# Grouped-query attention over a key and value cache on one core: the last row of wo's second half loaded by heads, and two V loads whole

## The chip, the core and the metric

The kernel runs on one of the eight cores of a Trainium2 chip. The metric is the device time of one execution in microseconds (us). A core has TensorE (PE, with its weight loads as PEld), VectorE (DVE), ScalarE (ACT), GpSimd (POOL) and SyncE (SP). SP and ACT issue the transfers from HBM, which 16 DMA engines carry out.

## The reference

Eight batches of four tokens ask 32 query heads, which share 8 heads of a cache of 2048 keys. All data is bf16.

```python
B, Sq, D = 8, 4, 512
Hq, Hkv, Sk, Dh = 32, 8, 2048, 128
q = (x @ wq).reshape(B, Sq, Hq, Dh).transpose(0, 2, 1, 3)
k = jnp.repeat(k_cache, Hq // Hkv, axis=1)
v = jnp.repeat(v_cache, Hq // Hkv, axis=1)
scores = jnp.einsum("bhqd,bhkd->bhqk", q, k) * (Dh ** -0.5)
p = softmax(scores)
o = jnp.einsum("bhqk,bhkd->bhqd", p, v)
out = o.transpose(0, 2, 1, 3).reshape(B, Sq, Hq * Dh) @ wo
```

k_cache and v_cache are 33.5 MB each, wq and wo 4.2 MB each.

## The kernel before

The work is cut into eight units `u`, each of which reads 4 MB of K and 4 MB of V. Units 1 to 6 (`single(u)`) are one batch with its eight heads; units 0 and 7 are four heads of the last two batches. All large loads go through `ring`, four slots of 4 MB, two members of 2 MB each. Loads are taken in the order k0, wq, k1, v0, k2, v1, ..., k7, v6, v7, wo, and a load goes into the slot of the load four before it, once that one's readers are done. `issue(done)` issues as many as fit; SP works them off in order, so a load that waits for its slot holds up the ones behind it. `load_kv` (L110) issues one load in parts: `by_member` makes two transfers of 2 MB, `whole` one of 4 MB, and `by_half` two of 2 MB, each with half of the keys of both members. The list `split` (L155) names the loads that go by member: V of units 0 to 4 and K of unit 7. V of unit 7 goes by half, the others are whole.

A unit runs so. DVE transposes K from the ring (`turn`, L213), PE multiplies it with the queries (`scores`, L251), DVE takes the maxima (`top`, L264), ACT the exponentials (L291), DVE turns them (L305), ACT, POOL and DVE copy them into a block-diagonal form (L315), and PE multiplies them with V (`values`, L331). Each matmul of L331 reads a key of both members of V at once. The result is scaled (L343, L351, L353), and PE orders it by tokens into a PSUM tile (`by_tokens`, L375).

The end is the product with wo. wo has 4096 rows of 512 numbers: 32 query heads of 128 rows. It comes as two halves `gg` of 16 heads, each into one member of the ring's slot. A partition holds 16 rows (`RW`), which are 16 successive rows of wo, so that eight partitions (`DG`) hold a head. `load_wo` (L141) issues the first half as one transfer of 2 MB, and the second in four parts by the rows of a partition, 0 to 7, 8 to 12, 13 and 14, and 15.

`to_rows(gg, n)` (L384) copies the attention output of a half out of PSUM (L389), and DVE transposes it, `n` rows at a time, into `oP[gg]` (L394): `oP[gg][:, r, :]` has, for each partition, the column of the output that belongs to its row `r` of wo. `project(gg, r0, r1)` (L399) then multiplies row after row, two matmuls each (L403), adding up in PSUM. The order at the end is: `to_rows(0, 16)` between the two parts of the last `values`; `project(0, 0, 4)`; `to_rows(1, 4)`, four transposes; `project(0, 4, 16)`; `project(1, 0, 16)`. Each row waits only for the transfer that has it and for its transpose. DVE and ACT then evict the two halves of the sum (L482, L483), and SP stores 32 KB (L484).

Of the kernel before, what the change touches and what calls it, by code (L numbers as in the profile page):

```python
# [17 lines left out]
def kernel(  # L18
# [9 lines left out]
    nc = tc.nc  # L28

    B, Sq, D = x.shape  # L30
    _, Hkv, Sk, Dh = k_cache.shape
    HqDh = wq.shape[1]
    Hq = HqDh // Dh
    rep = Hq // Hkv
    T = B * Sq
    R = D // 128
    G = 4
    S = 128 // G
    C = Sk // S
    NG = Hkv // G  # L40
    NB = 2
    NU = B * Hkv // (G * NB)
# [10 lines left out]
    DH = D // 2  # L53
    RW = 16
    DG = Dh // RW
    scale = float(Dh) ** -0.5
    assert Dh == 128 and C == 64 and Q == 16 and NB * Q == 32 and NT == 4 and NU == B == 8
    assert NS == NG == NB and NS1 == B - NB
# [14 lines left out]
    ring = ring_pool.tile([128, NR, NB, C * Dh], BF16, name="ring")  # L73
# [9 lines left out]
    oP = [const.tile([128, RW, T], BF16, name=f"oP{i}") for i in range(NG)]  # L83
# [17 lines left out]
    def take(key):  # L101
        slot_of[key] = n_loads[0] % NR
        n_loads[0] += 1
        return slot_of[key]
# [35 lines left out]

    def load_wo():  # L141
        slot = take("wo")
        for gg, cuts in ((0, (0, RW)), (1, (0, 8, 13, 15, RW))):
            rows = wo[gg * G * 512 : (gg + 1) * G * 512, :].rearrange("(p r) j -> p (r j)", r=RW)
            for r0, r1 in zip(cuts, cuts[1:]):
                nc.sync.dma_start(ring[:, slot, gg, r0 * D : r1 * D], rows[:, r0 * D : r1 * D])

    loads = ["k0", "wq", ("k", 1)]
    for u in range(NU):
# [2 lines left out]
            loads.append(("k", u + 2))  # L152
    loads.append("wo")
    loads.reverse()
    split = [("v", 0), ("v", 1), ("v", 2), ("v", 3), ("v", 4), ("k", NU - 1)]  # L155

    def issue(done):

        while loads and n_loads[0] < done + NR:
            what = loads.pop()  # L160
            if what == "k0":
                load_kv("k", 0, by_member, (nc.sync, nc.scalar))
                nc.sync.dma_start(x_sb[:, :], x.flatten_outer_dims())
            elif what == "wq":
                load_wq()
            elif what == "wo":
                load_wo()
            elif what in split:
                load_kv(*what, by_member)
            else:  # L170
                load_kv(*what, by_half if what == ("v", NU - 1) else whole)
# [11 lines left out]
    for r, b in ((r, b) for r in range(rep) for b in range(NB)):  # L183
        nc.gpsimd.tensor_copy(
            out=perm[:, r, W0 : W0 + 128]
            .rearrange("k (g x) -> k g x", g=G)[:, :, : NB * Sq]
            .rearrange("k g (b s) -> k b g s", b=NB)[:, b],
            in_=by_row[:, r, b],
        )
    for b in range(NB):  # L190
        nc.vector.tensor_reduce(
            out=of_b[:, b : b + 1],
            in_=ident[:, :].rearrange("k (g b q) -> k b g q", g=G, b=NB)[:, b],
# [190 lines left out]
    def to_rows(gg, n):  # L384

        o_r = q_sb[:, gg, :, :, :, :].rearrange("k r j w e -> k (r j w e)")
        half = rep * Dh // 2
        for i, copy in enumerate((nc.scalar.copy, nc.vector.tensor_copy)):
            copy(  # L389
                out=o_r[:, i * half : (i + 1) * half].rearrange("k (h d) -> k h d", d=Dh),  # L390
                in_=o_pms[i][:, :, gg, :],
            )
        for r in range(0, RW, n):
            nc.vector.transpose(  # L394
                out=oP[gg][:, r : r + n, :],
                in_=o_r.rearrange("k (h g r) -> k r h g", h=rep, r=RW)[:, r : r + n],
            )

    def project(gg, r0, r1):  # L399
        w = ring[:, slot_of["wo"], gg, :].rearrange("p (r j) -> p r j", r=RW)  # L400
# [19 lines left out]
    for gg in range(NG):  # L420
        psq = psum_o.tile([128, rep * Dh], FP32, tag="o", name="psq")
        for r in range(R):
# [10 lines left out]
            out=q_sb[:, gg, :, :, :, :].rearrange("t r j w e -> t (r j w e)"), in_=psq[:, :]  # L433
        )
        for i in range(rep):
            nc.vector.transpose(  # L436
                out=qT[:, gg, :, :, i, :, :].rearrange("w j b s e -> w j b (s e)").bitcast(FP32),
                in_=q_sb[:, gg, i, :, :, :].rearrange("t j w e -> t (j w e)").bitcast(FP32),
# [3 lines left out]
    for u in range(NU + 1):  # L442
# [19 lines left out]
        if u >= 1:  # L462
            values(u - 1, 0)
            if u == NU:
                joined(u - 2)
                by_tokens(u - 2)
                to_rows(0, RW)
            values(u - 1, 1)
            scaled(u - 1)
            if u == NU:  # L470
                joined(u - 1)
# [4 lines left out]
    project(0, 0, 4)  # L476
    by_tokens(NU - 1)
    to_rows(NG - 1, RW // 4)
    project(0, 4, RW)
    project(1, 0, RW)  # L480
# [34 lines left out]
```

## Time and profile before

| What | Value |
|---|---|
| Timed runs | 184.68, 190.56 and 191.4 us; median 190.56 us |
| Profiled execution | 184.38 us, of which the span of instructions 182.5 us |
| Busy: PE, DVE, ACT, POOL | 75%, 71%, 39%, 22% |
| Read from HBM | 75.53 MB, 414 GB/s over the span |
| DMA queues, share of 16 engines | SP's (q1) 94.3%, ACT's (q10) 2.8%, instructions (q8) 0.2% |
| Mean granted PE clock | 0.963 |
| wo's five transfers, KB and us to landing | 2048: 25.9, 1024: 28.2, 640: 29.1, 256: 29.3, 128: 28.0 |
| Store of the output | 32 KB, 1.5 us to landing |

The profile is one execution as the hardware profiler took it. Its span runs from the first to the last instruction; the rest of the execution's time lies around it. A line such as `L403 PE MATMUL s_ps<-ring,oP` is a line of the kernel, an engine, an operation, and the tiles that it writes and reads. In brackets behind it stands the time that the engine sat idle before it, and what ended that. A share of DMA is the mean busy share of the 16 engines in the stretch; a packet counts by its start, so a short stretch can show a little over 1. "Us to landing" runs from the issue of a transfer to its completion, so it has in it the time behind earlier transfers in the queue.

### The profile page before, as it was taken

The numbers are of one execution on the slowest core, as the hardware profiler recorded it, in microseconds if no ns is written. First come the engines' busy times: TensorE is split into PE (matmuls) and PEld (weight loads), VectorE is DVE, ScalarE is ACT, GpSimd is POOL, SyncE is SP. The second block draws the span as 40 slices with busy tenths as digits, with TensorE's granted clock in tenths as the row PEclk, the third lists the DMA queues.
The fourth block names the chain that finished last, engine by engine and source line by source line (L and its number), as shares of the span: only waits on it lengthen the run. The fifth ranks groups of instructions, "written<-read, shape, count | busy, mean of one in ns | idle before, by whom it ended". The sixth has DMA issues, their size and how long they took to land.

```text
span 182.5 us, 2386 instructions
## 1 busy us (share of the span) xinstructions
PE 136.6 (75%) x924; PEld 83.3 (46%) x924; DVE 128.7 (71%) x161; ACT 70.3 (39%) x91; POOL 39.3 (22%) x110
## 2 busy tenths in 40 slices
PE   0000076940999999998999898989399977899993
PEld 0000022310348635843783485358234852388971
DVE  6518025738994999599689957995399559967340
ACT  2000020019604940990395079109900792063010
POOL 8800006006200700430080035004400220023000
PEclk9999999995589999999999999999969999999999
DMA  6999999999999998999999999999999999999991
GB/s 226 431 485 395 424 460 406 424 445 449 452 384 427 456 461 382 420 460 452 391 417 453 460 402 418 431 478 424 391 435 424 435 427 435 415 426 438 427 385 42
DMA packets 4938, 75.70 MB, mean 415 GB/s; under 512 B 512, under 2 KB 704, under 8 KB 960
## 3 DMA queue, kind: packets, MB, share of 16 engines
q1 hardware_dynamic: 4784, 73.47, 94.3%
q10 hardware_dynamic: 144, 2.10, 2.8%
q8 instruction: 7, 0.11, 0.2%
q14 instruction: 3, 0.02, 0.0%
HBM read 75.53 MB, written 0.03 MB: 414 GB/s over the span
## 4 chain that ended last, share of the span: by engine, by line
DMA 42%; DVE 23%; PE 22%; issue 4%; ACT 3%; POOL 2%; SPq 1%; ACTq 0%; DVEq 0%; POOLq 0%
DMA ring<-in_wo_dram 16%; PE s_ps L251 16%; DMA ring<-in_k_cache_dram 15%; DVE kt L213 14%; DMA ring<-in_wq_dram 12%; DVE stat L264 4%; PE o_ps L331 4%; ACT p_sb L291 3%; PE psq L425 2%; DVE pt L305 2%; DVE stat L322 1%; POOL p_bd L315 1%; POOL q_bd L231 1%; PE s_ps L403 1%; DVE stat L272 0%
## 5 line engine op out<-in xcount | busy, mean ns | idle before, releaser
L251 PE MATMUL s_ps<-kt,q_bd 128*128 128x512 bf16 x256 | 69.5, 409 | 20.0 <-POOL q_bd L231 9.9
L213 DVE STREAM_TRANSPOSE kt<-ring 128x1024 f32<-128x1024 f32 x64 | 73.9, 1210 | 14.2 <-DMA ring<-in_k_cache_dram 11.4
L331 PE MATMUL o_ps<-ring,p_bd 128*128 128x256 bf16 x512 | 57.2, 273 | 0.0
L251 PEld LDWEIGHTS <-q_bd 128*128 128x128 bf16 x256 | 25.3, 102 | 63.0 <-issue 26.6
L331 PEld LDWEIGHTS <-p_bd 128*128 128x128 bf16 x512 | 49.8, 98 | 6.0 <-issue 0.2
L315 ACT COPY p_bd<-pt 32x1024 bf16<-32x1024 bf16 x44 | 45.8, 1041 | 1.5 <-DVE pt L305 1.1
L291 ACT ACTIVATE p_sb<-s_ps,stat 128x1024 bf16<-128x1024 f32 x16 | 17.7, 1110 | 72.2 <-DVE stat L272 72.2
L315 POOL COPY p_bd<-pt 32x1024 bf16<-32x1024 bf16 x16 | 17.0, 1065 | 105.9 <-DVE pt L305 93.2
L264 DVE TENSOR_REDUCE stat<-s_ps 128x1 f32<-128x1024 f32 x16 | 19.3, 1208 | 3.4 <-PE s_ps L251 3.4
L305 DVE STREAM_TRANSPOSE pt<-p_sb 128x512 f32<-128x512 f32 x16 | 11.4, 712 | 14.0 <-ACT p_sb L291 14.0
L231 POOL COPY q_bd<-qT 32x64 bf16<-32x64 bf16 x64 | 13.1, 231 | 20.7 <-DVE qT L436 19.0
L425 PE MATMUL psq<-ring,xT_sb 128*32 128x512 bf16 x32 | 3.6, 630 | 9.1 <-DMA ring<-in_wq_dram 9.1
L416 PE MATMUL xtp<-ident,x_sb 32*128 32x32 bf16 x4 | 0.3, 195 | 13.3 <-DMA x_sb<-in_x_dram 13.3
L436 DVE STREAM_TRANSPOSE qT<-q_sb 128x64 f32<-128x64 f32 x8 | 1.2, 214 | 8.8 <-ACT q_sb L432 8.8
L177 DVE MEMSET p_bd<- 128x2048 uint32 x3 | 5.3, 1765 | 2.0 <-PEq L499 1.2
L322 DVE TENSOR_SCALAR stat<-of_b,stat 128x2 f32<-128x2 f32 x8 | 6.3, 793 | 0.3
L416 PEld LDWEIGHTS <-x_sb 32*128 32x128 bf16 x4 | 0.2, 117 | 13.3 <-DMA x_sb<-in_x_dram 13.3
L425 PEld LDWEIGHTS <-xT_sb 128*32 128x32 bf16 x32 | 1.3, 140 | 10.5 <-issue 10.1
L432 ACT CAST q_sb<-psq 128x512 bf16<-128x512 f32 x2 | 1.2, 586 | 11.8 <-PE psq L425 11.8
L375 PEld LDWEIGHTS <-perm 128*128 128x128 bf16 x56 | 3.8, 97 | 2.0 <-issue 0.5
L419 ACT COPY xT_sb<-xtp 128x128 bf16<-128x128 bf16 x1 | 0.3, 266 | 11.2 <-PE xtp L416 11.2
L343 ACT ACTIVATE o_sb<-o_ps,stat 128x128 bf16<-128x128 f32 x8 | 2.9, 368 | 4.1 <-PE o_ps L331 3.9
(30 smaller groups left out, 46.4 us busy)
## 6 DMA issues: line engine op xcount, KB each, us to landing
ring<-in_k_cache_dram SPq DMA_DIRECT2D x6, 4096.0 KB, 22.7
ring<-in_v_cache_dram SPq DMA_DIRECT2D x12, 2048.0 KB, 23.6
ring<-in_v_cache_dram SPq DMA_DIRECT2D x2, 4096.0 KB, 29.6
ring<-in_k_cache_dram SPq DMA_DIRECT2D x3, 2048.0 KB, 27.2
ring<-in_wq_dram SPq DMA_DIRECT2D x1, 4096.0 KB, 21.0
ring<-in_k_cache_dram ACTq DMA_DIRECT2D x1, 2048.0 KB, 12.4
ring<-in_wo_dram SPq DMA_DIRECT2D x1, 2048.0 KB, 25.9
ring<-in_wo_dram SPq DMA_DIRECT2D x1, 1024.0 KB, 28.2
```

The costliest lines, as they stand in the source:

```text
L177: nc.vector.memset(t[:, :, :, :, :], 0.0)
L213: nc.vector.transpose(out=out, in_=in_)
L231: nc.gpsimd.tensor_copy(out=qb[k * 32 : (k + 1) * 32, m, :, g, b, :].rearrange("w (j e) q -> w j e q", e=2), in_=qT[of * 32 : (of + 1) * 3 ...
L251: nc.tensor.matmul(s_ps[t // 2][:, t % 2, :], lhsT=q_bd[u % 2][:, m, 2 * j + e, :, :, :].rearrange("w g b q -> w (g b q)"), rhs=rhs, start ...
L264: nc.vector.tensor_reduce(out=stats[u][0][:, h : h + 1], in_=s_ps[h][:, :, :].rearrange("q t n -> q (t n)"), axis=AX, op=ALU.max, negate=True,
L291: nc.scalar.activation(out=out, in_=in_, func=EXP, bias=stats[u][1][:, :], scale=scale, accum_out=stats[u][2][:, h : h + 1],)
L305: nc.vector.transpose(out=pt[:, :, :, :].rearrange("s c q e -> s (c q e)").bitcast(FP32), in_=ps[u, h][:, :, :, :].rearrange("q c s e -> q ...
L315: copy(out=pb[rows, :, g, :, :], in_=pt[rows, :, :, :])
L322: nc.vector.tensor_scalar_mul(stats[u][3][:, :], of_b[:, :], stats[u][4][:, :])
L331: nc.tensor.matmul(o_pss[u][:, :, :], lhsT=pbs[u, h][:, i // 2, :, :, i % 2].rearrange("s g q -> s (g q)"), rhs=v[:, :, key_of(u, h, i // ...
L375: nc.tensor.matmul(o_pms[r // 2][:, r % 2, gg, :], lhsT=perm[:, r, w : w + 128], rhs=o_sbs[u][:, b, :], start=(u == 0 and r % 2 == 0 and g ...
L425: nc.tensor.matmul(psq[g * T : (g + 1) * T, :], lhsT=xT_sb[:, r, :], rhs=w[:, (g * NB + gg) * rep * Dh : (g * NB + gg + 1) * rep * Dh], st ...
```

## The change

In wo's second half a head's 128 rows are given to its eight partitions in another way: each has 15 successive rows of the first 120 (`RL`), and as its sixteenth one of the head's last 8. Rows 0 to 7, 8 to 12, and 13 and 14 of the partitions still come as three transfers, from runs of 15 rows each. The sixteenth row comes by heads, where 8 rows of a head are one run of 8 KB in HBM and go to eight partitions: a transfer for heads 0 to 8, one for 9 to 13 and one for 14 and 15, in place of one for all partitions. The change's description says that these run on low DMA engines. `to_rows(1, 4)` follows: the transposes now take rows 0 to 3, 4 to 7, 8 to 11, 12 to 14, and 15. The first half of wo, its transfer and its transpose stay as they were. V of units 3 and 4 is no longer split, so each is one transfer of 4 MB.

```diff
+    RL = RW - 1
...
     def load_wo():
         slot = take("wo")
-        for gg, cuts in ((0, (0, RW)), (1, (0, 8, 13, 15, RW))):
-            rows = wo[gg * G * 512 : (gg + 1) * G * 512, :].rearrange("(p r) j -> p (r j)", r=RW)
-            for r0, r1 in zip(cuts, cuts[1:]):
-                nc.sync.dma_start(ring[:, slot, gg, r0 * D : r1 * D], rows[:, r0 * D : r1 * D])
+        half = wo.rearrange("(g k) j -> g (k j)", g=NG)
+        nc.sync.dma_start(ring[:, slot, 0, :], half[0].rearrange("(p n) -> p n", p=128))
+
+        heads = half[1].rearrange("(h n) -> h n", n=Dh * D)
+        runs = heads[:, : DG * RL * D].rearrange("h (i n) -> h i n", i=DG)
+        for r0, r1 in ((0, 8), (8, 13), (13, RL)):
+            nc.sync.dma_start(ring[:, slot, 1, r0 * D : r1 * D], runs[:, :, r0 * D : r1 * D])
+        for h0, h1 in ((0, 9), (9, 14), (14, 16)):
+            nc.sync.dma_start(
+                ring[h0 * DG : h1 * DG, slot, 1, RL * D :], heads[h0:h1, DG * RL * D :]
+            )
...
-    split = [("v", 0), ("v", 1), ("v", 2), ("v", 3), ("v", 4), ("k", NU - 1)]
+    split = [("v", 0), ("v", 1), ("v", 2), ("k", NU - 1)]
...
-        for r in range(0, RW, n):
-            nc.vector.transpose(
-                out=oP[gg][:, r : r + n, :],
-                in_=o_r.rearrange("k (h g r) -> k r h g", h=rep, r=RW)[:, r : r + n],
-            )
+        if gg == 0:
+            rows = [(r, r + n, o_r.rearrange("k (h i r) -> k r h i", h=rep, r=RW)[:, r : r + n]) for r in range(0, RW, n)]
+        else:
+            o_h = o_r.rearrange("k (h d) -> k h d", d=Dh)
+            runs = o_h[:, :, : DG * RL].rearrange("k h (i r) -> k r h i", i=DG)
+            rows = [(r, min(r + n, RL), runs[:, r : min(r + n, RL)]) for r in range(0, RL, n)]
+            rows.append((RL, RW, o_h[:, :, DG * RL :]))
+        for r0, r1, in_ in rows:
+            nc.vector.transpose(out=oP[gg][:, r0:r1, :], in_=in_)
```

## The prediction

> **What bounds the kernel now.** I read the page's shares and DMA queues first, then the chain that ended last, then the tail of the timeline, and last the DMA share in short stretches of the tail. Queues and issues first:
>
> ```profile
> DMA packets 4938, 75.70 MB, mean 415 GB/s; under 512 B 512, under 2 KB 704, under 8 KB 960
> ...
> q1 hardware_dynamic: 4784, 73.47, 94.3%
> q10 hardware_dynamic: 144, 2.10, 2.8%
> q8 instruction: 7, 0.11, 0.2%
> ...
> ring<-in_v_cache_dram SPq DMA_DIRECT2D x2, 4096.0 KB, 29.6
> ```
>
> The 16 DMA engines are busy for 94.3 + 2.8 = 97.1% of 182.5 us, while PE has 75% and DVE 71%. The kernel is a stream of 75.5 MB from HBM, with a start of some 3 us and a tail of some 3 us. A 4 MB transfer lands 29.6 us after its issue, though moving it takes 9.7 us, so the queue holds work far ahead and an earlier issue wins nothing. Seven packets of 16 KB (0.11 MB by 7) on q8 are instruction loads; 0.2% of 16 x 182.5 us is 5.8 us, or about 0.8 us for each (0.6 to 1.0 for the rounding), and each one holds up the engine that carries it.
>
> The chain of waits, cut to the end, and the timeline of the tail:
>
> ```profile
> 148.45 0.34 SPq L146
> 148.84 0.42 SPq L146
> 149.32 29.10 DMA ring<-in_wo_dram
> 178.46 0.27 PE s_ps L403
> ```
>
> ```profile
> 178.46 0.27 PE L403 MATMUL s_ps<-ring,oP 128*32 128x256 bf16 x1 [0.34 <-DMA ring<-in_wo_dram]
> ...
> 178.90 0.27 PE L403 MATMUL s_ps<-ring,oP 128*32 128x256 bf16 x1
> ...
> 179.09 0.27 PE L403 MATMUL s_ps<-ring,oP 128*32 128x256 bf16 x1
> ...
> 179.20 0.27 PE L403 MATMUL s_ps<-ring,oP 128*32 128x256 bf16 x1
> ...
> 179.39 0.27 PE L403 MATMUL s_ps<-ring,oP 128*32 128x256 bf16 x1
> ...
> 179.70 0.41 DVE L482 CAST out_sb<-s_ps 32x256 bf16<-32x256 f32 x1 [2.08 <-PE o_last L403]
> ...
> 180.17 0.35 SPq L484 DMA_DIRECT2D out_dram<-out_sb  x1
> ```
>
> The second half of wo comes in four parts (rows 0 to 7, 8 to 12, 13 and 14, row 15 of each partition). The first matmul of row 8 starts at 178.46, of row 13 at 179.09, of row 15 at 179.39: each is the landing of a part. Where nothing is waited for, a row follows the one before after 0.11 us (179.09, 179.20). So 2 rows of all partitions take 0.63 us to arrive and one row 0.30. From 179.39 the rest is fixed: evictions, a 32 KB store, the end at 182.5.
>
> Now the DMA share in stretches of 0.2 us. A line gives the stretch and its length, then busy time and count of PE, PEld, DVE, ACT and POOL, then PE clock, DMA share, GB/s:
>
> ```profile
> 177.40:177.60 0.20, 0.20 (x8) 0.20 (x5) 0.20 (x1) 0.00 (x0) 0.00 (x0) 1.00 0.87 338
> 177.60:177.80 0.20, 0.20 (x8) 0.20 (x6) 0.02 (x1) 0.00 (x0) 0.00 (x0) 1.00 0.65 246
> 177.80:178.00 0.20, 0.20 (x6) 0.14 (x3) 0.00 (x0) 0.00 (x0) 0.00 (x0) 1.00 0.55 205
> 178.20:178.40 0.20, 0.00 (x0) 0.00 (x0) 0.00 (x0) 0.00 (x0) 0.00 (x0) 1.00 0.41 159
> 178.60:178.80 0.20, 0.20 (x7) 0.20 (x5) 0.00 (x0) 0.00 (x0) 0.00 (x0) 1.00 0.44 154
> 178.80:179.00 0.20, 0.20 (x8) 0.20 (x3) 0.00 (x0) 0.00 (x0) 0.00 (x0) 1.00 0.20 67
> ```
>
> The engines don't stop together. Some run dry between 177.4 and 178.1, and then a share of 0.41 to 0.46 stays until 178.8: 7 of 16 is 0.44. So nine engines end early and seven about 0.9 us later, which is what seven instruction loads on seven engines would give. Packets end near 178.95 and the last landing is seen at 179.35, a lag of 0.4 us.
>
> **The change, part by part.** *Row 15.* A row of 128 partitions is 128 KB, 8 KB on each of 16 engines, 0.30 us. Instead, 16 runs of 8 KB (the last 8 rows of a head) go out as transfers of 9, 5 and 2 runs. If a transfer of n runs uses the n lowest engines, as the change's description says, engines 0 and 1 get three runs, 2 to 4 two, 5 to 8 one and the other seven none. [...]
>
> I take case one first: the seven late engines are the ones that get no run. They lose 0.30 us and end packets by 178.65, landing by 179.05. The early nine end at 177.1 to 177.8 after 15 rows, and with up to three runs (0.91 us) at 178.7 or before; landed by 179.1. So all of wo is there when rows 13 and 14 are, at 179.05. But row 15 still stands behind rows 13 and 14 on PE: 179.09, 179.20, then 179.31 in place of 179.39. The 0.30 us saved on the DMA side brings only **0.08 us**, since the landing of rows 13 and 14 on the late engines doesn't move.
>
> Case two: an engine among the lowest is late. It ends three runs minus one row later than now: 0.91 - 0.30 = 0.61, and row 15 starts at 180.00, **+0.61 us**. For a late engine that gets two runs +0.30; one run, 0. No view numbers the engines, so both ends stand: -0.08 and +0.61. I take the first: the early engines are nine and the first transfer has nine runs, so there is at least one assignment that fits exactly; the other end goes into the range.
>
> *Three waits for row 15* in place of one: two more semaphore instructions ahead of PE's matmul. PE's row isn't shown; DVE's own (L394 DVEq EVENT_SEMAPHORE) are 21 ns, so 2 x 0.02 = **+0.04 us**, from 0 if they are passed during rows 13 and 14. Behind them stand only the last two matmuls, and the evictions wait for these.
>
> *SP's issues.* Two more for wo, two fewer for V, so 32 transfers as before. They take eight semaphores in turn (the numbers stand in the trace's records of the issues), and one is issued when the eighth before it has landed: the transfer of 9 runs after the second half of the last K (150.1), that of 5 after V 6 (129.10 + 30.7 = 159.8), that of 2 after the first half of V 7 (137.43 + 27.2 = 164.6). An issue on this full queue took up to 4.81 us (L146's longest), so the last is out by 169.5 at worst; the engines need it from 177.4 on. Cover 8 us, cost 0. Nothing but the store (180.17) is queued behind it on SP.
>
> *V 3 and V 4 whole.* Every matmul of L331 reads both members, so PE can start no earlier with halves; L331 shows 0.0 us of idle time before it. The rate in the stretch of two halves of V 4 (111.10 to 120.80) is 451 GB/s, of whole V 5 433 and whole V 6 425, of the halves of V 3 443. These differ by the packets that start in a stretch (DMA shares 1.06, 1.01, 0.99, 1.04, over 1 for the same reason); per share they are 425, 429, 429 and 426. Cost 0. If the raw rates held, 2 x 4.19 MB would take 0.8 us more (19.4 against 18.6), which I keep as an upper bound.
>
> *Rows 0 to 14 by runs of 15*: same packet sizes (8, 5 and 2 KB), sources at 15 KB in place of 16: 0.
>
> *One transpose more* (L394: 4 of 0.37 us become 5, and with an odd stride). They end at 177.6 now; with 0.37 more, 178.0. Row 12 is needed at 178.90. Hidden; if the odd stride doubled them, 5 x 0.6 from 176.32 gives 179.3, +0.2 us.
>
> **The sum.** -0.08 + 0.04 = -0.04 us on a span of 182.5, so 182.45, and with the 1.9 us around it (184.38 - 182.5) **184.3 us**. That is against the profiled execution. The three timed runs are 184.68, 190.56 and 191.4, so the profiled one goes with the lowest and lies 3.2% under the median. No edit touches what could part them by 6 us.
>
> [...]
>
> **Rivals.** *A. The low engines are late* (slower): engine 0 or 1 carries an instruction load and three runs. Price +0.61, with waits +0.65: 185.0 us. It decides once any engine's delay plus its runs passes the delay of the seven by one row, 0.30 us. For: nothing shows the numbers. Against: seven of sixteen are late, and nine can take the runs. Chance 0.18.
>
> *B. Small transfers pay a fixed time each*, one after the other on engine 0. The store, 32 KB on an idle queue, takes 1.5 us from issue to landing. Three such after 177.8 would end at 182.3, row 15 three us later: 187.4. [...] Against it: the 0.30 us between the landings of two parts. Chance 0.05.
>
> *C. The change doesn't do what it says*: the runs of a transfer go through one engine. 9 x 0.30 = 2.7 us after 178.7, with the lag 181.8: +2.4, 186.8 us. Or PE's order alone hides everything: 184.4, as good as the forecast. Chance 0.07.
>
> *D. The measurement, not the change*: 184.7 and 191 are two groups of the same kernel, and a median of few runs can fall in either. Beside a median of 190.56, 184.3 would read as -3.3%, and the reverse as +3.4%. Chance 0.22: 0.17 for the first (the median stands in the upper group), 0.05 for the second.
>
> **How the numbers follow.** The forecast keeps 0.48. It, A, B and C all lie within 2% (3.7 us, about what a measurement of this kernel can tell from no change): 0.48 + 0.18 + 0.05 + 0.07 = 0.78; I move 0.01 of it to slower, for B with more. So faster 0.17, within 2% 0.77, slower 0.06. The forecast's own range, beside the profiled run, is 183.9 to 185.2; to hold the upper group of times, which is as likely for the changed kernel as for this one, the range is 183.7 to 191.5.
>
> **What would show it.** wo in seven transfers, of which 72, 40 and 16 KB; V with four whole ones. The last matmul start after row 14 by 0.11 us without a wait; the DMA share after 178.0 near 0.7 to 0.9 and then falling at once, in place of the step at 0.44. A step that lasts past 179 with a share near 0.06 to 0.13 (one or two engines) is A or C. Wrong would be a span that moves by over 1 us, or V's whole loads with another rate or a wait of L331.

## The result and the profile after

The changed kernel is slower: its time is 1.0251 times that of the kernel before, with a 95% interval of 1.0204 to 1.0298. Two of its six runs and four of the six of the kernel before fell into a second, slower state and are left out of this ratio; with them the medians stand the other way round, 189.4 us after (188.58 to 195.45) and 190.44 us before (184.41 to 193.44). The profiled executions are 188.58 us with a span of 186.9, and 184.38 with 182.5, so 4.4 us of span are to be found.

The page of the changed kernel, its GB/s in 40 slices of 4.7 us and its queues:

```profile
GB/s 235 435 459 449 442 407 396 438 449 449 396 435 449 423 428 419 424 480 428 389 428 456 449 395 435 445 435 410 435 431 424 435 428 426 423 428 430 237 213 12
...
q1 hardware_dynamic: 4752, 73.47, 93.8%
```

The same bytes move at the same rate for 37 slices. Then come two slices at 237 and 213 GB/s, and the engines are hardly less busy in them (9 and 8 tenths of these slices, 9 before). Up to the end of V nothing differs: the second half of V 7 is issued at 140.07 and lands 29.5 us later, at 169.57; before, 139.94 and 29.6. Nearly all that is lost lies in wo. Its issues, size and time to landing, in the changed kernel:

```profile
ring<-in_wo_dram SPq DMA_DIRECT2D x1, 2048.0 KB, 27.4
ring<-in_wo_dram SPq DMA_DIRECT2D x1, 1024.0 KB, 31.2
ring<-in_wo_dram SPq DMA_DIRECT2D x1, 640.0 KB, 33.1
ring<-in_wo_dram SPq DMA_DIRECT2D x1, 256.0 KB, 33.1
```

Before they were 25.9, 28.2, 29.1 and 29.3. Rows 0 to 7 (1024 KB) take 3.0 us longer and rows 8 to 12 take 4.0 us longer. The first half of wo, whose transfer is the same in both kernels, takes 1.5 us longer too. The chain that ended last shows the same step as before, longer:

```profile
148.58 0.34 SPq L145
...
148.97 0.68 SPq L150
...
149.71 33.10 DMA ring<-in_wo_dram
...
182.85 0.27 PE s_ps L415
```

And PE's timeline with what it waited for:

```profile
176.06 0.27 PE L415 MATMUL s_ps<-ring,oP 128*32 128x256 bf16 x1 [1.55 <-DMA ring<-in_wo_dram]
...
177.57 1.32 DVE L409 STREAM_TRANSPOSE oP<-q_sb 128x128 bf16<-128x128 bf16 x5
...
180.18 0.27 PE L415 MATMUL s_ps<-ring,oP 128*32 128x256 bf16 x1 [1.76 <-DMA ring<-in_wo_dram]
...
182.85 0.27 PE L415 MATMUL s_ps<-ring,oP 128*32 128x256 bf16 x1 [1.62 <-DMA ring<-in_wo_dram]
...
183.43 0.27 PE L415 MATMUL s_ps<-ring,oP 128*32 128x256 bf16 x1
...
183.54 0.27 PE L415 MATMUL s_ps<-ring,oP 128*32 128x256 bf16 x1
...
183.65 0.27 PE L415 MATMUL s_ps<-ring,oP 128*32 128x256 bf16 x1
```

PE waits for the first half of wo (176.06), for rows 0 to 7 (180.18) and for rows 8 to 12 (182.85). Rows 13, 14 and 15 then follow each other by 0.11 us: row 15 comes with no wait of its own, as forecast, but 4.26 us later than before. Of these, 4.04 us are the last landing of wo, that of rows 13 and 14 (183.39; before, row 15's at 179.35), and 0.22 us are the two rows on PE ahead of row 15.

The DMA share and GB/s (last two columns) in three of these microseconds, first before, then after:

```profile
174.00:177.00 3.00, 2.65 (x41) 2.02 (x39) 1.45 (x5) 0.74 (x2) 0.00 (x0) 1.00 0.99 407
```

```profile
174.00:177.00 3.00, 1.45 (x19) 0.92 (x19) 0.35 (x1) 0.44 (x2) 0.00 (x0) 1.00 0.94 229
177.00:180.00 3.00, 1.42 (x25) 1.15 (x25) 1.74 (x6) 0.30 (x1) 0.00 (x0) 1.00 0.97 238
```

The engines are busy, 0.94 and 0.97 against 0.99, at little more than half the rate. So each packet takes longer: by the trace's packet records, the 128 packets of 8 KB have a median of 523 ns (before, all take 309), those of 5 KB 321 (196), those of 2 KB 129 (84). The first half of wo is caught as well: of its 16 completion records, which I read as one for each engine, ten come by 173.93 and six from 175.36 on, and its last six packets of 16 KB take 1162 to 1268 ns in place of 611, though this transfer has the old form. 2.1 MB at 407 GB/s are 5.2 us, at 234 GB/s 9.0: 3.8 us, nearly all of the 4.04 us by which the last landing moved (179.35 to 183.39).

### The profile page after: what moved, and what is told of

It is laid out like the page before. It is cut to its first block, busy times and chain, and to the rows that moved or that the text cites. A ratio compares the mean times of both kernels' runs of the same rounds, so it can differ in the third digit from the quotient of the medians.

```text
span 186.9 us, 2388 instructions
## 1 busy us (share of the span) xinstructions
PE 136.8 (73%) x924; PEld 83.3 (45%) x924; DVE 128.7 (69%) x162; ACT 70.2 (38%) x91; POOL 39.1 (21%) x110
## 4 chain that ended last, share of the span: by engine, by line
DMA 44%; DVE 22%; PE 22%; issue 4%; ACT 3%; POOL 2%; SPq 1%; ACTq 0%; DVEq 0%; POOLq 0%
DMA ring<-in_wo_dram 18%; PE s_ps L259 15%; DMA ring<-in_k_cache_dram 15%; DVE kt L221 14%; DMA ring<-in_wq_dram 11%; DVE stat L272 4%; PE o_ps L339 4%; ACT p_sb L299 3%; PE psq L437 2%; DVE pt L313 2%; DVE stat L330 1%; POOL p_bd L323 1%; POOL q_bd L239 1%; PE s_ps L415 1%; DVE stat L280 0%
## 5 line engine op out<-in xcount | busy, mean ns | idle before, releaser
L415 PE MATMUL s_ps<-ring,oP 128*32 128x256 bf16 x32 | 4.2, 272 | 4.9 <-DMA ring<-in_wo_dram 4.9
L415 PEld LDWEIGHTS <-oP 128*32 128x32 bf16 x64 | 3.2, 96 | 5.7 <-issue 5.5
## 6 DMA issues: line engine op xcount, KB each, us to landing
ring<-in_wo_dram SPq DMA_DIRECT2D x1, 2048.0 KB, 27.4
ring<-in_wo_dram SPq DMA_DIRECT2D x1, 1024.0 KB, 31.2
```

Of the source, the lines that this page charges most:

```text
L415: nc.tensor.matmul(out_ps[half], lhsT=oP[gg][:, r, :], rhs=w[:, r, half * DH : (half + 1) * DH], start=(gg == 0 and r == 0), stop=(gg == N ...
```

## The experiments

Four theories for the lost time, the first three for the slow packets; each is a guess of mine, to be tested. **P**: the source of rows 0 to 14 has two steps (16 heads, 8 runs each). If the transfer is then dealt out to the engines by heads, each engine gets eight neighbouring partitions, and engines may meet where they write. **Q**: a step of 15 KB in HBM is slow to read. **R**: the transfers by heads slow the rest. **S**: the whole V loads cost it.

**V whole, alone** (on the kernel before):

```diff
-    split = [("v", 0), ("v", 1), ("v", 2), ("v", 3), ("v", 4), ("k", NU - 1)]
+    split = [("v", 0), ("v", 1), ("v", 2), ("k", NU - 1)]
```

> The kernel before with V of units 3 and 4 whole, and nothing else of the change. In the changed kernel the last of V lands at 169.57 us of the span, before at 169.53, so the loss of 4.4 us lies behind it, in wo. Theories P (the two-step source of wo's rows 0 to 14 gives each DMA engine the eight neighbouring partitions of a head, so that engines meet at the same partitions' side of the memory), Q (the step of 15 rows, 15 KB, in HBM is slow to read) and R (the small transfers by heads slow the others): all say no change, span 182.5 within 0.5. Theory S (whole V loads cost time): +4 us.

Ratio 1.0012, interval 0.9997 to 1.0027; profiled span 182.7. Its 640 KB of wo take 29.1 us to landing, as before. S falls.

**One even step of 15 rows** (on the changed kernel):

```diff
-        runs = heads[:, : DG * RL * D].rearrange("h (i n) -> h i n", i=DG)
+        runs = half[1][: 128 * RL * D].rearrange("(p n) -> p n", p=128)
...
-            nc.sync.dma_start(ring[:, slot, 1, r0 * D : r1 * D], runs[:, :, r0 * D : r1 * D])
+            nc.sync.dma_start(ring[:, slot, 1, r0 * D : r1 * D], runs[:, r0 * D : r1 * D])
```

> The changed kernel, but rows 0 to 14 of a partition come from one even step of 15 rows over all 128 partitions (the first 1920 rows of the half), so a part's source has one step in place of two (16 heads by 8 runs). It reads other rows of wo than the reference asks for. P: wo at the full rate of 420 GB/s or more, span back to 182.2 to 182.8. Q: still 15 KB steps, so 210 to 250 GB/s in the tail and a span of 186 to 187. R: also 186 to 187.

> The changed kernel with rows 0 to 14 from one even step of 15 rows once more, for a second profile (other rows of wo than the reference asks for). P: span 182.5 to 183.2, 8 KB packets 309 ns, 9.8 to 10.3 us from the end of V to the last landing of wo. The transfers by heads are in it: their share is what is left over the kernel before, 0 to 0.6 us.

The fastest of its runs is 184.86 us, against 184.27 for the fastest of the kernel before; its span is 183.1, 0.3 us over what P had said. Both profiled executions have longer spans than expected (187.4 and 188.3), but there V had ended 4.4 and 5.5 us later already, ahead of all that was edited, so I read them from the end of V on. The last of wo lands 10.2 and 10.0 us behind it (kernel before 9.8, changed kernel 13.8), and all 128 packets of 8 KB take 309 ns in both. The tail of the second:

```profile
179.50:182.50 3.00, 2.72 (x43) 2.10 (x42) 1.47 (x5) 0.74 (x2) 0.00 (x0) 1.00 0.99 404
```

404 GB/s with a step of 15 KB and with the transfers by heads in place: Q and R fall.

**Two steps with 16 KB between runs** (on the kernel before, no transfer by heads):

```diff
+            if gg == 1:
+                rows = bass.AP(wo.tensor, G * 512 * D, [[(Dh - 1) * D, 16], [RW * D, DG], [1, RW * D]])
...
```

> The kernel before, but the four parts of wo's second half read with two steps: 16 heads at 127 rows, 8 runs each at the old 16 rows (16 KB). 127 in place of 128 keeps the two steps from being one; it reads other rows of wo than the reference asks for. No transfer by heads, V as before. P: the tail slows as in the changed kernel, 210 to 250 GB/s, span 186 to 187.5. Q: 16 KB steps as before, span 182.5. R: 182.5.

Ratio 1.0288, interval 1.0235 to 1.034; 189.3 us the fastest of five. Issues, and the DMA share in the tail of its profiled execution (there V ended 6.9 us late, so the stretch lies later):

```profile
ring<-in_wo_dram SPq DMA_DIRECT2D x1, 1024.0 KB, 31.3
ring<-in_wo_dram SPq DMA_DIRECT2D x1, 640.0 KB, 33.0
```

```profile
181.00:184.00 3.00, 1.34 (x18) 0.83 (x17) 0.36 (x2) 0.49 (x2) 0.00 (x0) 1.00 0.92 223
```

31.3 and 33.0 us are the changed kernel's 31.2 and 33.1, and the last of wo lands 13.8 us behind the end of V, as there. A step of 127 rows from head to head in place of 128, by which the source keeps two steps, brings the whole loss alone. That leaves P, or a simpler theory **T**: any source of two steps is slow. Two kernels set them apart, one with one step where by P engines should meet, one with two steps where by P they should not.

**One step, 64 partitions at a time** (on the kernel before, full computation):

```diff
-                nc.sync.dma_start(ring[:, slot, gg, r0 * D : r1 * D], rows[:, r0 * D : r1 * D])
+                for p0, p1 in ((0, 128),) if gg == 0 else ((0, 64), (64, 128)):
+                    nc.sync.dma_start(ring[p0:p1, slot, gg, r0 * D : r1 * D], rows[p0:p1, r0 * D : r1 * D])
```

> The kernel before, but each of the four parts of wo's second half goes as two transfers, one of partitions 0 to 63 and one of 64 to 127; one even step of 16 rows. Theory P (engines meet because each one's partitions are neighbours on sides of the memory that another engine is writing): 64 partitions on 16 engines give four neighbouring ones to each, and pairs of engines meet, so 8 KB packets take 450 to 620 ns as in the changed kernel (median 518) and wo takes 13 us or more from the end of V to its last landing (changed kernel 13.8, before 9.8). Theory T (any source of two steps is slow, whatever the partitions): one step here, so 309 ns and 9.8 to 10.2 us.

The profiled span is 188.5, with V ending at 169.5 as before, so the 6.0 us are the tail's. The last landing has 5.1 of them (184.43 against 179.35); most of the rest is PE's, whose granted clock was 0.50 from 180 us on, where a row took 0.21 us in place of 0.11. The first lines of the tail:

```profile
174.00:177.00 3.00, 1.01 (x14) 0.61 (x12) 0.35 (x1) 0.37 (x1) 0.00 (x0) 1.00 1.01 214
177.00:180.00 3.00, 2.86 (x28) 1.77 (x28) 1.71 (x5) 0.37 (x1) 0.00 (x0) 0.57 0.94 213
```

Full engines (1.01, 0.94) at 214 and 213 GB/s, half of what they do in the kernel before (407); 8 KB take a median of 596 ns in place of 309. One even step is slow here, so two steps are not needed for the loss.

**Two steps, eight groups of four partitions** (on the kernel before; rows 0 to 7 of partitions 64 to 127 left out):

```diff
+                if gg == 1 and r0 == 0:
+                    for p0 in (0, 32):
+                        of = bass.AP(
+                            wo.tensor, (G * 512 + p0 * RW) * D, [[(4 * RW - 1) * D, 8], [RW * D, 4], [1, r1 * D]]
+                        )
+                        nc.sync.dma_start(ring[p0 : p0 + 32, slot, gg, : r1 * D], of)
+                    continue
```

> The kernel before, but rows 0 to 7 of wo's second half come as two transfers of 32 partitions, each with a source of two steps (8 groups at 63 rows, 4 partitions each at 16 rows); rows 0 to 7 of partitions 64 to 127 are left out, so 0.5 MB less is moved, and other rows than the reference's are read. Eight groups mean eight engines, each with a group of four partitions of its own that no other writes. P: no two meet, so these 64 packets of 8 KB take 309 to 330 ns in spite of the two steps. T: about 518 ns.

V ended 5.5 us later in this profiled execution, so the stretch lies later:

```profile
178.00:181.00 3.00, 2.71 (x30) 2.15 (x27) 0.45 (x2) 0.37 (x1) 0.00 (x0) 1.00 0.92 380
```

380 GB/s at a share of 0.92 is 413 at a full one, no less than the 407 of the kernel before, and all 64 packets of 8 KB take 309 ns. Each of the two transfers leaves eight completion records, so by my reading of them it uses eight engines; that each of these has a group of partitions to itself is P's assumption. Two steps are not slow in themselves: T falls, and so far P stands.

The trace shows how many completion records a transfer leaves, not which partitions an engine writes. That part of P was my assumption, and the kernels above agree with it without showing it. So P's place of meeting is argued, not shown. The trace of the changed kernel shows no pairs of engines that hold each other up: packets of 8 KB that start at about the same time take about the same time (the ten that start from 175.0 to 175.2 us take 461 to 493 ns, the eight from 176.0 to 176.2 take 589 to 627). Nor is a conflict on the side of HBM excluded: if they are dealt out by heads, engines read 128 KB apart (127 with the step of 127 rows), and no run changes that distance alone. Against it speaks the run by 64 partitions, which is slow with the old even step.

**Row 15 on few engines, and nothing else**, was asked in two ways. First row 15 by heads, rows 0 to 14 as before (row 15 is then another row of wo than the reference's):

```diff
+                if r1 == RW and r0 > 0:
+                    continue
...
+        heads = wo.rearrange("(g h k) j -> g h (k j)", g=NG, k=Dh)[1]
+        for h0, h1 in ((0, 9), (9, 14), (14, 16)):
+            nc.sync.dma_start(
+                ring[h0 * DG : h1 * DG, slot, 1, (RW - 1) * D :], heads[h0:h1, (Dh - DG) * D :]
+            )
```

> The kernel before, rows 0 to 14 as before, and only row 15 in three transfers by heads (9, 5 and 2 runs of 8 KB). Row 15 of a partition is then another row of wo than the reference asks for. P and Q: the tail keeps its rate; the span moves as the prediction's sum or its rival A said, -0.1 to +0.65 us: 182.4 to 183.1. The three parts' landings tell which: all before or with those of rows 13 and 14 if the seven late engines are not among the lowest nine. R: 186 to 187.

Span 183.1, 0.6 us over before, the rate kept. Only part of the 0.6 us is wo's: V ends 0.17 us later, and the last landing comes 10.1 us behind it in place of 9.8. Then by groups of partitions, with the whole computation:

```diff
-                nc.sync.dma_start(ring[:, slot, gg, r0 * D : r1 * D], rows[:, r0 * D : r1 * D])
+                groups = ((0, 128),) if r1 < RW or r0 == 0 else ((0, 63), (63, 98), (98, 123), (123, 128))
+                for p0, p1 in groups:
+                    nc.sync.dma_start(ring[p0:p1, slot, gg, r0 * D : r1 * D], rows[p0:p1, r0 * D : r1 * D])
```

> The kernel before with the whole computation, V split as before, and row 15 of wo's second half in four transfers of 63, 35, 25 and 5 partitions, each with one even step: the lightening of some engines without the change's other layout. If transfers take the lowest engines (9, 7, 5, 5), the seven highest get none of row 15. P: the rate of wo stays, 9.6 to 10.2 us from the end of V to the last landing, span 182.3 to 183.1, no change that 2% could show. If the last part lands by 0.4 us or more after rows 13 and 14, a late engine is among the lowest.

Ratio 1.0036, interval 1.0007 to 1.0065: 0.13 to 1.2 us slower, so no gain either. The profiled span of 183.4 is 0.3 us over what was expected. The last part of row 15 lands 0.34 us behind rows 13 and 14 (179.94 and 179.60), just short of the 0.4 us that was to be the sign of a late engine among the lowest; the records of the two kernels say more. In the first, the transfer of nine runs ends last, at 179.78 by the completion records. Eight of its nine records come by 178.8, and one 1.0 us after these: by the reading of a record as an engine, a late engine is among those nine. The transfers of 5 and 2 runs end at 179.14 and 179.21, so it is one of the engines with a single run, if all three transfers use the same lowest engines. In the second, the transfers with nine and seven records end last, each with two records 0.7 us or more behind its others. But rows 13 and 14, which were not touched, land late too: 9.9 and 9.8 us behind the end of V against 9.5.

Why these rows are late was asked with half of row 15 left out:

```diff
-                nc.sync.dma_start(ring[:, slot, gg, r0 * D : r1 * D], rows[:, r0 * D : r1 * D])
+                p0, p1 = (0, 128) if r1 < RW or r0 == 0 else (0, 63)
+                nc.sync.dma_start(ring[p0:p1, slot, gg, r0 * D : r1 * D], rows[p0:p1, r0 * D : r1 * D])
```

> The kernel before, but row 15 of wo's second half comes for partitions 0 to 62 alone, in one transfer (63 partitions, so nine engines); the other 65 partitions' row 15 is left out. It asks why e4_heads and e6_row15 landed rows 13 and 14 0.5 us later than the kernel before, though these rows were not touched. Theory M (the early engines' writes of row 15 meet those of late engines, which are still writing rows 13 and 14, and the late engines are those of partitions 64 to 127): here the early ones write only partitions 0 to 62, so rows 13 and 14 keep 84 ns a packet of 2 KB, and land as before, 9.5 us after the end of V. Theory N (transfers on fewer than 16 engines delay a landing in themselves): 9.8 to 9.9 us, as in e4_heads and e6_row15.

and the same with `(64, 127)`:

> The same with partitions 64 to 126 alone, in one transfer on the same nine engines; row 15 of the other 65 partitions is left out. M: the early engines now write where the late ones do, so many packets of 2 KB take 95 to 160 ns, and rows 13 and 14 land 9.7 to 10.0 us after the end of V. N: the same as in e8_row15_first.

Rows 13 and 14 land 9.7 us behind the end of V in both: over M's 9.5 for the first half, the lowest that M allowed for the second, and under N's 9.8 to 9.9. Of the 128 packets of 2 KB, 3 and 1 take over 88 ns (45 with row 15 by heads, 30 by groups, none before). So M, with the late engines at partitions 64 to 127, is not borne out, and N is not met. With all of row 15 on few engines a quarter to a third of these packets is slowed, with half of it almost none; why stays open.

No version that does the whole computation ran faster than the kernel before.

## Why the prediction was wrong, point by point

- **The step that failed** is the shortest of the sum: "*Rows 0 to 14 by runs of 15*: same packet sizes (8, 5 and 2 KB), sources at 15 KB in place of 16: 0." The sizes are indeed the same and the 15 KB cost nothing (404 GB/s with one even step). What I passed over is that an even step over 128 partitions became 16 steps by 8. It measured +4.0 us at the last landing and, alone on the kernel before, a ratio of 1.0288. That the second step brings the loss here is shown by the runs; that the engines get in each other's way is argued.
- **The sign of being wrong** that was named, a span that moves by over 1 us, came: 4.4 us. That the range of 183.7 to 191.5 holds 188.58 us is luck: it was made that wide for rival D, not for a slower wo.
- **No rival had it.** All four left the rate of the large transfers alone; I looked at the 128 KB that change engines and not at the 1920 KB beside them. A fair bound would have asked what the slowest transfer with the same packet sizes could do.
- **The number of engines** was right, a completion record read as an engine: the three transfers leave 9, 5 and 2 records. Which engines these are no view shows, so that they are the lowest, on which the -0.08 us rests, is not shown. The transfers of rows 0 to 14 leave 16 records each, before and after, so in the number of engines the loss could not be seen.
- **Row 15, -0.08 us**: wrong in sign as far as the two kernels with row 15 on few engines show (the last landing 0.3 to 0.4 us later behind the end of V; 1.0036 by groups). The term of the sum took it that rows 13 and 14 land as before; they landed 0.3 to 0.4 us late. Rival A named another reason, a late engine among the lowest nine, and gave +0.65 for engine 0 or 1. By the records there was one, with a single run if the three transfers share their lowest engines, as priced at 0: by heads, row 15 starts at 179.84, 0.1 us behind row 14 and with no wait, so that engine cost nothing. In the changed kernel itself the three transfers land by 182.93, ahead of rows 13 and 14.
- **PE's order** was right: row 15 follows rows 13 and 14 by 0.11 us each with no wait (183.43, 183.54, 183.65).
- **V whole, 0**: right, 1.0012. The raw rates' upper bound of 0.8 us (a ratio of 1.004) lies outside the interval.
- **SP's issues, 0**: right. The transfers of 9, 5 and 2 runs went out at 152.68, 159.81 and 164.74 (forecast from 150.1, 159.8, 164.6).
- **The transposes**: five in 1.32 us, from 1.29 for four, and hidden: they end at 178.89, and the row that needs the first of them waits for wo until 180.18.

## What to carry to other kernels

When a transfer's source changes from one step to two, measure that load alone before building on it, though bytes and packet sizes stay: here it cost 0.4 of the rate (229 to 238 GB/s in place of 407), while with two steps over groups of four partitions nothing was lost (380 GB/s at a share of 0.92). A busy share of 0.94 to 0.97 beside little more than half the GB/s meant here that the packets themselves took longer, and packet times (8 KB in 523 ns in place of 309) showed it at once. One even step over all 128 partitions kept the rate in these runs (404 to 407 GB/s, with 15 KB and with 16); two transfers of 64 partitions with the same even step did not (214).

## What the runs showed of the hardware that was not expected

- The transfers of 64 partitions ran at 214 GB/s, those of 128 at 407, though the engines were busy (share 1.01).
- In the changed kernel the first half of wo, whose transfer is the same in both kernels and which stands ahead of those of two steps in the queue, landed 27.4 us after its issue in place of 25.9.
- With the 128 KB of row 15 on transfers of nine completion records and fewer in place of 16, rows that nobody touched landed 0.3 to 0.4 us later behind the end of V (9.9 and 9.8 us against 9.5).
